# Forward and backward of a memory-augmented recurrent transformer block on one core: memory rows in another buffer, the last rest rows summed earlier, pinned GpSimd copies, one store on another queue

## Chip, core and metric

The kernel runs on one core of a Trainium2 chip. The metric is the device time of one execution in microseconds (us). Three executions of the kernel before took 2919.24, 2901.86 and 2914.58 us; their median is 2914.58 us. Three executions of one program thus lie up to 0.6% apart.

Engines are called as in the profile: PE is TensorE's matmul side, PEld its weight loads, DVE is VectorE, ACT is ScalarE, POOL is GpSimd, SP is SyncE. SP computes nothing here; it issues DMAs. POOL computes and also issues DMAs. Each engine takes its instructions strictly in the order in which they stand in its queue, so an instruction that waits holds up everything behind it.

## What is computed

One pre-LayerNorm block and the gradients of its inputs and weights, in bf16: 2048 tokens of width D = 448. The attention runs over 64 segments of 32 tokens, one after the other. Each segment sees its own tokens and 8 memory rows, and the first 8 output rows are the memory of the next segment. After that come a second LayerNorm and a SwiGLU feed-forward part (FFN) of width 1792.

```python
def _A_ref(x, mem0, Wq, Wk, Wv, Wo, seg_len):      # 16 heads of 256, M = 8, seg_len = 32
    mem = mem0
    for s in range(n_seg):                          # 64
        h = jnp.concatenate([mem, x[:, s*seg_len:(s+1)*seg_len, :]], axis=1)
        q, k, v = (jnp.einsum('btd,dhe->bhte', h, W) for W in (Wq, Wk, Wv))
        scores = jnp.where(mask, jnp.einsum('bhqe,bhke->bhqk', q, k) * scale, -1e9)
        o = jnp.einsum('bhqk,bhke->bhqe', _softmax(scores), v)
        o = jnp.einsum('bhte,hed->btd', o, Wo)
        mem = o[:, :M, :]
        outs.append(o[:, M:, :])
    return jnp.concatenate(outs, axis=1)
...
h  = x + _A_ref(_layernorm(x), mem0, Wq, Wk, Wv, Wo, 32)
h2 = h + (silu(_layernorm(h) @ w_gate) * (_layernorm(h) @ w_up)) @ w_down
# results: h2 and the gradients of x, mem0, Wq, Wk, Wv, Wo, w_gate, w_up, w_down for grad_out
```

## The kernel before

The program has four stages, which follow each other on PE. Their places in the profiled execution are: forward chain 0 to about 953 us, FFN forward and backward to about 1268, backward chain over the segments to about 2222, and the weight gradients (the tail) to the end.

A tile framework orders the instructions. It sorts by a priority, the chains stand in a high-priority block, and `tc.issue_after(ins)` puts an instruction no earlier than another one. The framework also adds the semaphore waits: for data, for a buffer that is still read or written, and for the semaphore of an earlier DMA, since each queue's DMAs take turns on eight semaphores.

**Forward chain** (lines 398 to 903). Each segment projects q, k and v, does the softmax and the output projection, and saves its tiles to DRAM. Some transposed weights are also made for later: `piece()` loads a block of a weight transposed into one of two staging buffers (`stg_b`), and `save()` notes a store of that buffer for later. `save_all(last)` issues the noted stores: on POOL's queue when `last` is None, else on SP's queue behind the segment's other stores. In the last segment (`end`) the two staging buffers are used once more, as `last_x`: `turned_by_pe` (line 618) turns the last token block on PE and copies four PSUM banks into them. The store that still reads one of them is that of a block of Wv turned (`Tv`, line 566). Also in the last segment, `_FFNLoads.at(0)`, `at(1)` and `at(2)` issue the loads of the FFN's weights on SP.

**FFN** (lines 906 to 1129). Eight iterations of two 128-token tiles. In each, PE does the gate, up and `dz` projections (`proj`, line 988), the down projection (1086), and the input gradient (1112). `sg` holds the sigmoids. POOL then makes `t1 = 1 - sg` over 3584 elements per partition (`k.pool_op`, line 1063), which DVE needs (1068, 1075) before its products (1093 to 1095), which in turn the matmuls of line 1112 read. `normed(n + 1)` (line 1011) prepares the next iteration: it normalises the rows (1018) and pads the loaded `grad_out` rows from 448 to 512 columns by a small copy on POOL (1020). `load_in` (299) fetches those rows on SP.

**Backward chain** (lines 1132 to 1600). 64 segments in reverse order, about 14 us each, in tiles t of four segments (r = s mod 4 runs 3, 2, 1, 0). What bears on the change:

- SP issues, in this order for each segment: the loads of the next one (`load_rest` 1201, `load_p` 1209, `load_v` 1213, `load_qk` 1221), then `own_saved` (1372), and once a tile, at r = 3, `prep_tile(t - 1)` (1170). `prep_tile` loads the output gradients of the next tile, turned, into the buffer `dhx`.
- The same buffer `dhx` also holds `rO`, and, once every 16 segments (jm == 0, that is s = 48, 32, 16 and 0), the rows of the memories' gradients, `rows` (line 1556). `memory_rows` (376) stores them by four DMAs on POOL's queue (381).
- A tile's rest rows (the first 8 of every segment) are projected as a list of small matmuls, `parts`, into the bank `pX`, copied to `om2`, summed over four groups of columns (`summed`, 1339; `rest_out`, 1356), copied to `pxs` and stored to `DXN` by four DMAs (`rest_sums_saved`, 1374).
- With all rows of `DXN` there, `norm_load` (1362), `norm_first` (1379) and `norm_second` (1392) do the LayerNorm's backward for the tile: loads of `DXN` into `om2`, of `XN` into `xn_t` and of `DH` into `dh_h`, then ACT and DVE work, and a store of `xn_t` to the result. `om2`, `xn_t` and `dh_h` are single buffers. `norm_first` writes a product it doesn't need into `prod_t`.
- After the loop, tile 1 and tile 0 are left (lines 1585 to 1595). Tile 1 goes through its LayerNorm part first; then tile 0's rest rows are summed and it goes through its own.

**Tail** (lines 1603 to 1810). Sums of outer products over all rows. The first group (`rows_by_d`, 1722) fills five `psf` banks and one `fx` bank with 20 matmuls each; ACT and DVE copy the banks out (lines 75 and 76), and the next group uses them again.

Of the kernel before, what the change touches and what calls it, by code (L numbers as in the profile page):

```python
# [10 lines left out]
BF16 = mybir.dt.bfloat16  # L11
# [379 lines left out]
def forward_chain(k: _K):  # L391
    nc, tc = k.nc, k.tc
    S, D, M, H, Dh, HD = k.S, k.D, k.M, k.H, k.Dh, k.HD
    SEG, L, NSEG, NT, KC, DP, MC, DC = k.SEG, k.L, k.NSEG, k.NT, k.KC, k.DP, k.MC, k.DC
# [39 lines left out]
    om = k.f32("f3", 256, "om")  # L434
# [134 lines left out]
    def save_all(last=None):  # L569
        for i in (1, 2):  # L570
            for fn in unsaved.pop((rot[0] + i) % 2, ()):
                if last is None:
                    fn()
                else:
                    with tc.issue_after(last.ins):
                        fn(nc.sync)
# [80 lines left out]
    def residual(t, h_t, x_t, last_v):  # L657
        with tc.issue_after(last_v.ins):
            nc.vector.tensor_tensor(out=h_t, in0=h_t, in1=x_t, op=ALU.add)
        nc.gpsimd.dma_start(out=dr["Hh"][t * P:(t + 1) * P, :], in_=h_t)  # L660
        st = smal.tile([P, nc.vector.BN_STATS_DIM], FP32, name="stats")
        with tc.issue_after(last_v.ins):
            nc.vector.bn_stats(out=st[:], in_=h_t)
        nc.vector.bn_aggr(out=k.mv2[:, t, :], in_=st[:])
# [7 lines left out]
    for s in range(NSEG):  # L672
        t, r = divmod(s, 4)
# [4 lines left out]
        xblk, om2 = xblk_b[t % 2], om_b[s % 2]  # L678
        end = s == NSEG - 1
        if due and jm % 3 == 1 and jm > 3:  # L680
            fetch(due[0], h_t, x2_t)
        with k.prio.crit():
# [146 lines left out]
            else:  # L829
                pm = k.ps1()  # L830
                for c in range(2):
# [3 lines left out]
                    out=hT_roll[:, :, (s + 1) % NWIN, SEG:L].rearrange("p (d c) m -> p d c m", d=2),  # L835
                    in_=pm[:, 0:32].rearrange("p (c d m) -> p d c m", c=2, d=2))
# [9 lines left out]
        for g in range(2):  # L846
            v_out = nc.sync.dma_start(out=dr["VG"][s, L * g:L * g + L], in_=Vs[64 * g:64 * g + L, :])
# [8 lines left out]
        if due and jm % 3 == 0 and jm > 5:  # L856
            n = due.pop(0)
            residual(n, h_t, x2_t, to_v)
        save_all(v_out)
        if (r == 0 and t > 0) or s == 2:  # L860
            prep_tile(t + 2)
        if s >= 4 and ((r > 0 and jm < 15) or (jm == 0)):
# [32 lines left out]
        elif jm == 15:  # L895
            for hf in range(2):
# [3 lines left out]
                                        in_=mh.rearrange("p c n -> p (c n)"))  # L900
# [10 lines left out]
def ffn_phase(k: _K, back):  # L911
    nc, tc = k.nc, k.tc
    S, D, F = k.S, k.D, k.F
    SEG, NT, KC, DP, FC = k.SEG, k.NT, k.KC, k.DP, k.FC
# [11 lines left out]
    h_b, dout_b, load_in = fl.h_b, fl.dout_b, fl.load_in  # L926
# [74 lines left out]
    last = NT // G - 1  # L1001
# [9 lines left out]
    def normed(n, after):  # L1011
        for tt in range(G):
            t = G * turns[n] + tt
            i = 2 * (n % 2) + tt
            for o, c0 in ((0, 0), (D, D - 64)):
                w = D if o == 0 else 64
                with tc.issue_after(after.ins):
                    nc.vector.tensor_scalar(out=hn_b[i][:, o:o + w], in0=h_b[i][:, c0:c0 + w], scalar1=mv2[:, t, 0:1],
                                            scalar2=rstd2[:, t:t + 1], op0=ALU.subtract, op1=ALU.mult)
            nc.gpsimd.tensor_copy(out=dout_b[i][:, D:DP], in_=dout_b[i][:, D - 64:D])  # L1020
            nc.gpsimd.dma_start(out=dr["HN"][t * P:(t + 1) * P, :], in_=hn_b[i][:, 0:D])

    def turned(n):
# [10 lines left out]
    for n, gi in enumerate(turns):  # L1034
# [44 lines left out]
        for tt in range(G):  # L1079
            t = G * gi + tt  # L1080
            rows = slice(t * P, (t + 1) * P)
# [20 lines left out]
        for tt in range(G):  # L1102
            t = G * gi + tt
            rows = slice(t * P, (t + 1) * P)
# [4 lines left out]
            i = 0  # L1109
# [16 lines left out]
        if n == last:  # L1126
            for tt in range(G):
                t = G * gi + tt
# [4 lines left out]
def backward_chain(k: _K):  # L1133
    nc, tc = k.nc, k.tc
    S, D, M, H, Dh, HD = k.S, k.D, k.M, k.H, k.Dh, k.HD
    SEG, L, NSEG, NT, KC, DP, MC, DC = k.SEG, k.L, k.NSEG, k.NT, k.KC, k.DP, k.MC, k.DC
# [5 lines left out]
    DQ = D // 4  # L1142
# [14 lines left out]
    dhx = A(59.8125, 4, P)  # L1157
    dOr = A(62.0625, 5, P)
    dxs, pxs = [x.bitcast(FP32) for x in (B(10.125, 2 * DQ), A(63.3125, 2 * DQ))]
# [92 lines left out]
    for c in range(4):  # L1252
        d0 = DQ * c
        while d0 < DQ * (c + 1):
            n = min(DQ * (c + 1), (d0 // P + 1) * P) - d0
# [11 lines left out]
    prod_t = k.f32("f2", D, "prod")  # L1267
    prod = prod_t[:, 0:8 * L].rearrange("p (h n) -> p h n", n=L)
    rO = dhx.rearrange("p c n -> p (c n)")
    om, om2 = k.f32("f1", 512, "om"), k.f32("f3", D, "om2")  # L1270
    dO_own = om[:].bitcast(BF16)
    pX, pD, pH = k.bank(6), k.bank(5), k.bank(7)
    with k.prio.crit():
        for b in range(2):
            pr, src = k.bank(b), (rO, A(46, 512))[b]
# [61 lines left out]
    def summed(ps, part):  # L1337
        for q in range(4):
            last = nc.tensor.matmul(ps[32 * q:32 * q + 32, 0:DQ], lhsT=sel[:], rhs=part[:, DQ * q:DQ * q + DQ],
                                    start=True, stop=True, skip_group_check=True)  # L1340
        return last

    parts = []

    def rest_parts(n):
        last = None
        for _ in range(min(n, len(parts))):
            last = parts.pop(0)()
        return last
# [6 lines left out]
    def rest_out():  # L1356
        summed(pX, om2)
        nc.scalar.copy(out=pxs, in_=pX[:, 0:DQ])
# [3 lines left out]
    def norm_load(t):  # L1362
        x = norm[t] = [om2, None]
        rows = slice(t * P, (t + 1) * P)
        nc.gpsimd.dma_start(out=x[0][:], in_=dr["DXN"][rows])
        nc.gpsimd.dma_start(out=xn_t, in_=dr["XN"][rows, 0:D])
        for c0 in (0, 224):
            nc.gpsimd.dma_start(out=dh_h[c0 // 224], in_=dr["DH"][rows, c0:c0 + 224])

    def own_saved(s):  # L1370
        r0 = 32 * s + M
        nc.sync.dma_start(out=dr["DXN"][r0:r0 + 32].rearrange("n (q d) -> q n d", q=4), in_=dxs)

    def rest_sums_saved(t):
        dst = dr["DXN"][t * P:(t + 1) * P].rearrange("(r n) (q d) -> q r n d", r=4, q=4)
        for q in range(4):
            nc.gpsimd.dma_start(out=dst[q][:, 0:M], in_=pxs[32 * q:32 * q + 32])

    def norm_first(t, after):
        x, rstd, junk = norm[t][0], k.rstd1[:, t:t + 1], prod_t  # L1380
        m1, m2 = [smal.tile([P, 1], FP32, name=f"lnb_m{i}") for i in (1, 2)]
        with tc.issue_after(after["s"].ins):
            nc.scalar.activation(out=x[:], in_=x[:], func=ACT.Copy, accum_out=m1[:])
        nc.vector.tensor_tensor_reduce(out=junk[:, 0:D], in0=x[:], in1=xn_t, scale=1.0, scalar=0.0,
                                       op0=ALU.mult, op1=ALU.add, accum_out=m2[:])
        m1s, m2s = [smal.tile([P, 1], FP32, name=f"lnb_m{i}s") for i in (1, 2)]
        nc.vector.tensor_scalar(out=m1s[:], in0=m1[:], scalar1=-1.0 / D, scalar2=rstd, op0=ALU.mult, op1=ALU.mult)
        nc.vector.tensor_scalar(out=m2s[:], in0=m2[:], scalar1=-1.0 / D, scalar2=None, op0=ALU.mult)
        nc.vector.scalar_tensor_tensor(out=x[:], in0=xn_t, scalar=m2s[:], in1=x[:], op0=ALU.mult, op1=ALU.add)
        norm[t][1] = m1s  # L1390

    def norm_second(t, after):
        x, m1s = norm.pop(t)
        with tc.issue_after(after["s"].ins):
            nc.scalar.activation(out=x[:], in_=x[:], func=ACT.Identity, scale=k.rstd1[:, t:t + 1], bias=m1s[:])
        for c0 in (0, 224):
            nc.vector.tensor_tensor(out=xn_t[:, c0:c0 + 224], in0=x[:, c0:c0 + 224], in1=dh_h[c0 // 224], op=ALU.add)
        nc.gpsimd.dma_start(out=OUT1[t * P:(t + 1) * P, :], in_=xn_t)

    V_FILL = {3: 16, 2: 16, 1: 16, 0: 3 * MC}  # L1400
    for s in range(NSEG - 1, -1, -1):
        t, r = divmod(s, 4)
# [14 lines left out]
        with k.prio.crit():  # L1417
# [6 lines left out]
            pool_op = nc.gpsimd.tensor_copy(out=doT[:, :, 0:M], in_=R4_b[t % 2][:, :, r * M:(r + 1) * M])  # L1424
# [78 lines left out]
            def first_rows(nm):  # L1503
                last = {}
                for b in range(3):
                    c0, n, v = c12(pps[nm][b], b)
                    with tc.issue_after(turned["vsv"[b]].ins):
                        last["vsv"[b]] = k.evac(lo[nm][:, c0:c0 + n, r * M:(r + 1) * M], v[:, :, 0:M], "vsv"[b])
                return last
# [8 lines left out]
            cast = first_rows("q")  # L1518
# [20 lines left out]
            pool_op = nc.gpsimd.tensor_copy(out=dmr[0:DQ, :, jm, :], in_=do_roll[0:DQ, :, sl, SEG:L])  # L1539
# [6 lines left out]
            if s > 0:  # L1546
# [3 lines left out]
                                      in_=pm[0:DQ, 0:P].rearrange("p (c n) -> p c n", n=32)[:, :, 24:32])  # L1550
# [2 lines left out]
                    nc.sync.dma_start(out=OUT2[:, DQ * q:DQ * q + DQ], in_=ot[32 * q + 24:32 * q + 32, :])  # L1553
            nc.scalar.copy(out=dxs, in_=pq[:, 0:DQ])
            if jm == 0:
                rows = dhx.rearrange("p c n -> p (c n)")
                k.evac(rows[:, 0:D], pr[:, 0:D], "s")
            if rest:
                k.evac(rO, pR[:], "s")
# [8 lines left out]
        if r == 0:  # L1568
# [10 lines left out]
            for fn, at in due:  # L1579
                if s == 0:  # L1580
                    k.last_stores.append(fn)
                else:
                    later(s - at[0], at[1], fn)
    own_saved(0)
    for t in (1, 0):
        if t == 0:
            rest_parts(len(parts))
            nc.scalar.copy(out=om2[:], in_=pX[:, 0:D])
            rest_out()
        with tc.issue_after(pool_op.ins):  # L1590
            rest_sums_saved(t)
            norm_load(t)
        norm_first(t, cast)
        norm_second(t, cast)
    assert not pending


# [243 lines left out]
```

## Time and profile before

| what | value |
|---|---|
| median of three executions | 2914.58 us |
| the profiled execution | 2902.99 us, of which the span in the trace is 2901.2 us |
| PE busy | 94% of the span, 41647 matmuls |
| DVE, ACT, POOL busy | 45%, 36%, 32% |
| DMA | 571.55 MB, 197 GB/s on average; the software queue (POOL's) 157.95 MB, the hardware queue (SP's) 407.32 MB |
| mean granted PE clock | 0.981 of full speed |

Times in the trace count from the start of the span. A line of a timeline gives the start, the time, the engine and source line, what it writes and reads, how many instructions were merged, and in brackets how long the engine had been idle and what ended that. A line of the list of waits gives who waited for whom, then the total in us, how often, and the longest wait. "SPq" is SP's DMA queue: the time there is how long SP took to issue.

### The profile page before, as it was taken

How to read it: one execution, taken by the hardware profiler on the slowest of the kernel's cores; microseconds unless marked ns; L12 is line 12 of the kernel's file. 1: busy time of each engine (PE TensorE's matmuls, PEld its weight loads, DVE VectorE, ACT ScalarE, POOL GpSimd, SP SyncE). 2: the span in 40 equal slices, each digit the busy share in tenths (PEclk: the TensorE clock that was granted, in tenths of full speed). 3: DMA queues.
4: the chain of work that ended last, by engine and by line, in shares of the span. 5: the costliest groups of instructions: out<-in, count | busy, mean ns of one | idle time of the engine just before them, and what ended most of it. 6: DMA issues, size and time to landing. Idle time of an engine off the chain costs nothing.

```text
span 2901.2 us, 98006 instructions
## 1 busy us (share of the span) xinstructions
PE 2737.4 (94%) x41647; PEld 1579.0 (54%) x41651; DVE 1306.1 (45%) x3352; ACT 1046.3 (36%) x2579; POOL 925.1 (32%) x2064
## 2 busy tenths in 40 slices
PE   5999999999999998989999999999998989999999
PEld 3565556565555555545565555555554444544444
DVE  4555565555555576645554554555553011111110
ACT  2555455455454444433333333333332011111110
POOL 1222232233222222423554544545543111111211
PEclk9999999999999999989999999999999999999999
DMA  7677778777777989995776777776778997969951
GB/s 259 149 190 196 193 189 200 192 191 198 202 184 213 290 202 225 213 301 142 172 186 173 177 175 179 179 180 166 179 171 264 322 248 159 215 175 229 184 165 52
DMA packets 781870, 571.55 MB, mean 197 GB/s; under 512 B 632432, under 2 KB 673688, under 8 KB 778872
## 3 DMA queue, kind: packets, MB, share of 16 engines
q1 hardware_dynamic: 717224, 407.32, 59.6%
q0 software_dynamic: 64208, 157.95, 17.3%
q8 instruction: 328, 5.37, 0.8%
q14 instruction: 110, 0.90, 0.1%
HBM read 181.58 MB, written 244.92 MB: 147 GB/s over the span
## 4 chain that ended last, share of the span: by engine, by line
PE 72%; DMA 10%; issue 7%; ACT 3%; DVE 3%; SPq 2%; POOL 2%; POOLq 0%; ACTq 0%; DVEq 0%
PE bank L1333 9%; PE psf L1682 8%; PE psf L590 6%; PE psf L725 5%; PE bank L1180 4%; PE po L772 4%; PE psf L988 3%; PE fx L1682 3%; PE bank L1298 2%; PE psf L614 2%; PE fx L1112 2%; PE bank L1353 2%; DMA arA<-VG 2%; PE bank L1439 2%; PE psf L506 2%
## 5 line engine op out<-in xcount | busy, mean ns | idle before, releaser
L75 DVE CAST arA<-psf 128x512 bf16<-128x512 f32 (+2 forms) x285 | 159.8, 561 | 487.6 <-PE psf L1682 249.9
L76 ACT CAST arA<-psf 128x512 bf16<-128x512 f32 (+3 forms) x379 | 189.7, 509 | 524.1 <-PE psf L1682 215.2
L1333 PE MATMUL bank<-arW,arA 128*32 128x448 bf16 x6144 | 319.6, 356 | 7.0 <-DMA arW<-Tq 3.6
L76 ACT CAST arA<-bank 128x96 bf16<-128x96 f32 (+4 forms) x608 | 193.5, 376 | 108.3 <-PE bank L1321 90.5
L1682 PEld LDWEIGHTS <-arA 128*128 128x128 bf16 x1440 | 139.4, 99 | 162.4 <-issue 7.7
L1682 PE MATMUL psf<-arW,arA 128*128 128x512 bf16 x882 | 224.4, 383 | 0.0
L1333 PEld LDWEIGHTS <-arA 128*32 128x32 bf16 x6144 | 155.4, 97 | 125.8 <-ACT arA L76 12.2
L725 PE MATMUL psf<-arW,arA 128*64 128x512 bf16 x1536 | 212.2, 382 | 0.0
L590 PE MATMUL psf<-arW,arA 128*32 128x512 bf16 x3072 | 189.8, 381 | 7.8 <-DVE arA L75 0.9
L988 PE MATMUL psf<-arW 128*128 128x256 bf16 (+1 forms) x1288 | 149.0, 277 | 5.9 <-DVE arA L75 4.6
L1759 POOL DMA_DIRECT2D out_dram<-arA x96 | 52.0, 542 | 261.6 <-DVE arA L75 234.9
L1210 POOL DMA_DIRECT2D arA<-P_all x256 | 127.7, 505 | 22.3 <-issue 17.9
L988 PEld LDWEIGHTS <-arW 128*128 128x128 bf16 (+1 forms) x1344 | 103.3, 97 | 57.8 <-issue 46.3
L75 DVE CAST arA<-bank 128x256 bf16<-128x256 f32 (+4 forms) x386 | 129.4, 389 | 9.1 <-PE bank L1180 4.2
L1180 PE MATMUL bank<-arW,arA 112*32 112x512 bf16 x2048 | 131.4, 400 | 1.6 <-DVE arA L1549 1.6
L772 PE MATMUL po<-arW,arA 128*32 128x256 bf16 (+1 forms) x4096 | 128.3, 263 | 1.2 <-DVE arA L75 1.2
L590 PEld LDWEIGHTS <-arA 128*32 128x32 bf16 x3072 | 70.3, 96 | 105.2 <-issue 28.5
L1722 PE MATMUL psf<-arW 128*128 128x448 bf16 x525 | 112.9, 357 | 5.1 <-DVE arA L75 5.1
L772 PEld LDWEIGHTS <-arA 128*32 128x32 bf16 x4096 | 104.7, 96 | 9.0 <-DVE arA L75 1.5
L1226 POOL COPY arB<-arB 40x320 bf16<-40x320 bf16 x128 | 64.4, 503 | 117.3 <-DMA arB<-P_all 81.8
L76 ACT CAST arB<-psf 128x64 bf16<-128x64 f32 (+1 forms) x192 | 65.1, 341 | 98.1 <-PE psf L597 75.7
L1112 PE MATMUL fx<-arW,arA 128*128 128x448 bf16 x448 | 89.2, 358 | 10.2 <-DVE arW L1088 10.2
(316 smaller groups left out, 5079.7 us busy)
## 6 DMA issues: line engine op xcount, KB each, us to landing
arW<-T SPq DMA_DIRECT2D x256, 128.0 KB
X_o<-arA SPq DMA_DIRECT2D x37, 512.0 KB
T<-arA SPq DMA_DIRECT2D x64, 256.0 KB
X_v<-arA POOLq DMA_DIRECT2D x30, 512.0 KB
X_k<-arA POOLq DMA_DIRECT2D x30, 512.0 KB, 4.5
X_q<-arA POOLq DMA_DIRECT2D x30, 512.0 KB, 3.2
out_dram<-arA POOLq DMA_DIRECT2D x84, 128.0 KB, 4.8
VG<-arA SPq DMA_DIRECT2D x64, 160.0 KB
```

The lines of the kernel that those rows point to most:

```text
L75: return nc.vector.tensor_copy(out=out, in_=in_)
L76: return nc.scalar.copy(out=out, in_=in_)
L590: nc.tensor.matmul(banks[b][w][32 * q:32 * q + 32, :], lhsT=hT_roll[:, kc, sl, M:L], rhs=(Wq_sb, Wk_sb)[w][:, kc, col(q, b)], start=(b == ...
L725: nc.tensor.matmul(pV[b][64 * g:64 * g + 64, 0:512], lhsT=hT_flat[:, kc, sl * L:sl * L + 64], rhs=Wv_sb[:, kc, n * 512:(n + 1) * 512], sta ...
L772: last = nc.tensor.matmul(pO[32 * q:32 * q + 32, 0:w], lhsT=xblk[:, j, r * SEG:(r + 1) * SEG], rhs=Wo_sb[:, cj(j), 256 * dh:256 * dh + w], ...
L988: nc.tensor.matmul(ps[fp][:, f2 * 256:(f2 + 1) * 256], lhsT=Wt[lo:hi, kc, c * P:(c + 1) * P], rhs=xT[lo:hi, kc, :], start=(kc == 0 and f2 ...
L1112: k.last_dh = nc.tensor.matmul(pdh[:, 0:D], lhsT=srcT[:, tt, c, :], rhs=WT[:, c, :], start=(i == 0), stop=(i == 2 * FC - 1))
L1180: last = nc.tensor.matmul(bank[32 * q:32 * q + 32, :], lhsT=lhs(c), rhs=WoT_sb[0:DQ, c, n0:n0 + 512], start=(c == 0), stop=(c == 3), skip_ ...
L1210: nc.gpsimd.dma_start(out=P4[32 * q:32 * q + 32, 2 * x + g], in_=pa[64 * g + M:64 * g + L, x])
L1333: last = nc.tensor.matmul(ps[32 * q:32 * q + 32, 0:D], lhsT=lhs(j), rhs=WT[:, cj(j), :], start=(start and i < 4), stop=(stop and i >= len( ...
L1682: k.last_mm = nc.tensor.matmul(pa[i][:, 0:w], lhsT=lhs_of(b)[:, i // 2 * P:(i // 2 + 1) * P], rhs=rhs_of(q, b, i % 2), start=(b == 0), sto ...
L1722: k.last_mm = nc.tensor.matmul(pa[i][:, 0:D], lhsT=lhs_of(b, i), rhs=rhs_of(b), start=(bi == 0), stop=(bi == m + 3))
```

## The change

Four edits in one diff:

1. The memory rows go into `om2` (seen as bf16) and no longer into `dhx`, except in segment 0. The four stores of `memory_rows` then read `om2`.
2. After the loop, the rest of `parts` is run first, `pX` is copied to `om` (no longer `om2`), summed, and copied to the first 112 columns of `prod_t`. Both tiles' rest sums are stored, tile 1's from `pxs` and tile 0's from `prod_t`. After that, both tiles go through their LayerNorm parts, pinned behind that last copy on ACT.
3. In the FFN, the padding copies of `normed(n)` for n > 0 are pinned behind POOL's `t1` operation of the iteration that calls them.
4. In the last forward segment `save_all` issues the noted store on POOL's queue and not behind the segment's stores on SP.

```diff
@@ forward_chain
-        save_all(v_out)
+        save_all(None if end else v_out)
@@ ffn_phase, normed(n, after)
-            nc.gpsimd.tensor_copy(out=dout_b[i][:, D:DP], in_=dout_b[i][:, D - 64:D])
+            with tc.issue_after(k.pool_op.ins) if n > 0 else nullcontext():
+                nc.gpsimd.tensor_copy(out=dout_b[i][:, D:DP], in_=dout_b[i][:, D - 64:D])
@@ backward_chain
-    def rest_sums_saved(t):
+    def rest_sums_saved(t, src=pxs):
         dst = dr["DXN"][t * P:(t + 1) * P].rearrange("(r n) (q d) -> q r n d", r=4, q=4)
         for q in range(4):
-            nc.gpsimd.dma_start(out=dst[q][:, 0:M], in_=pxs[32 * q:32 * q + 32])
+            nc.gpsimd.dma_start(out=dst[q][:, 0:M], in_=src[32 * q:32 * q + 32])
...
             if jm == 0:
-                rows = dhx.rearrange("p c n -> p (c n)")
+                rows = om2[:].bitcast(BF16) if s > 0 else dhx.rearrange("p c n -> p (c n)")
                 k.evac(rows[:, 0:D], pr[:, 0:D], "s")
...
     own_saved(0)
+    rest_parts(len(parts))
+    nc.scalar.copy(out=om[:, 0:D], in_=pX[:, 0:D])
+    summed(pX, om)
+    last = {"s": nc.scalar.copy(out=prod_t[:, 0:DQ], in_=pX[:, 0:DQ])}
+    for t, src in ((1, pxs), (0, prod_t[:, 0:DQ])):
+        with tc.issue_after(pool_op.ins):
+            rest_sums_saved(t, src)
     for t in (1, 0):
-        if t == 0:
-            rest_parts(len(parts))
-            nc.scalar.copy(out=om2[:], in_=pX[:, 0:D])
-            rest_out()
-        with tc.issue_after(pool_op.ins):
-            rest_sums_saved(t)
-            norm_load(t)
-        norm_first(t, cast)
-        norm_second(t, cast)
+        norm_load(t)
+        norm_first(t, last)
+        norm_second(t, last)
     assert not pending
```

## The prediction

> **What bounds the kernel now.** I read the page first, then PE's list of waits, then the timelines around each long wait.
>
> ```profile
> PE 2737.4 (94%) x41647; PEld 1579.0 (54%) x41651; DVE 1306.1 (45%) x3352; ACT 1046.3 (36%) x2579; POOL 925.1 (32%) x2064
> ...
> PE bank L1315 <- DMA arA<-P_all: 11.9, 6, 4.3
> PE fx L1112 <- DVE arW L1088: 10.2, 3, 7.3
> PE bank L1339 <- ACT om L1588: 7.9, 1, 7.9
> PE psf L1722 <- DVE arA L75: 5.1, 1, 5.1
> PE psf L988 <- DVE arA L75: 4.6, 1, 4.6
> ```
>
> PE bounds the kernel: it is idle for 2901.2 − 2737.4 = 164 us only. No edit removes matmuls, so all that can be won lies in these waits and in the slow clock behind them. The five are in the places that the change touches.
>
> **Memory rows.** This is the timeline of SP, POOL and PE around the end of segment 48.
>
> ```profile
> 1513.46 1.75 POOL L381 DMA_DIRECT2D DC<-arA  x3 [0.33 <-issue]
> ...
> 1516.42 0.58 SPq L1372 DMA_DIRECT2D DXN<-arB  x1
> 1520.43 1.22 SPq L1170 DMA_TRANSPOSE arA<-DHb  x1
> ...
> 1523.96 4.55 SPq L1209 DMA_DIRECT2D arA<-P_all  x8
> ...
> 1530.13 0.42 PE L1315 MATMUL bank<-arA 32*128 32x160 bf16 x2 [4.28 <-DMA arA<-P_all]
> ```
>
> SP is free at 1517.00, but `prep_tile` (1170) starts at 1520.43: it may not write `dhx` before the four stores of line 381 have read it. Behind it on SP stand the loads of the next segment, so PE waits 4.28 us for the P rows. The granted clock from 1531 to 1536 is then 0.50. By the starts of line 1545, segments 46, 30 and 14 take 20.63, 19.41 and 20.10 us, where an undisturbed one at r = 2 takes 13.74: 18.9 us lost in all. With the rows in `om2` SP's waits go (3.4, 2.5 and 3.4 us). The stores themselves stay, at the same place on POOL; `om2`'s next writer is the `DXN` load at 1523.74, after the stores have landed (5 to 6 us after issue), so nothing new waits there. PE's idle times of 4.28, 4.05 and 4.10 fall to about 0.9, 1.5 and 0.7, which is 3.1 us left. What is late next is the same load of P rows. Short gaps can cost clock too: after gaps of 0.91, 1.96 and 1.32 us (segments 24, 18, 7) the clock was 0.62, 0.71 and 0.64, and about 2.2 us more were lost; after 0.87 (segment 42) it stayed at 1.00. Of the three gaps left I count one as followed by such a loss, 2 us. **Gain 18.9 − 3.1 − 2 = 14 us**; ends 18.9 (no gap left) and 18.9 − 3.1 − 6.6 = 9.
>
> [...]
>
> **Pinned pool copies.** Timelines of POOL, DVE and PE in the FFN's fourth iteration:
>
> ```profile
> 1094.14 0.24 POOL L1020 COPY arW<-arW 128x64 bf16<-128x64 bf16 x1 [3.13 <-DMA arW<-in_grad_out_dram]
> 1094.34 3.17 POOL L1063 TENSOR_SCALAR arW<-arA 128x3584 bf16<-128x3584 bf16 x1
> ...
> 1097.55 2.03 DVE L1068 TENSOR_TENSOR arW<-arA,arW 128x3584 bf16<-128x3584 bf16 x1 [9.88 <-POOL arW L1063]
> ...
> 1105.23 7.50 PE L1112 MATMUL fx<-arW,arA 128*128 128x448 bf16 x28 [7.31 <-DVE arW L1088]
> ```
>
> The copies for the next iteration stand ahead of `t1` on POOL and wait for their load; `t1` was ready at about 1080.6, when ACT ended the sigmoids. Pinned behind it, `t1` ends near 1084, DVE's 1068 follows its own 1058 at 1087.7, the products start when ACT has the last `dz` (1093.1) and end before PE is through line 1086 (1097.9): no wait is left. That is 7.31 us, and 28 matmuls in 7.50 us instead of the 5.46 of other iterations, 2.04. Two more iterations have waits of 1.45 (at 1061.75 and 1180.27) with the same cause. Sum 12.2. The moved copies (0.24 us each, two per iteration) now hold up POOL's stores behind them; these wait for DVE until 8 to 11 us later anyway. PE turns the copied rows about 20 us after `t1`'s start. Against it: the FFN's DMA share is 0.9 to 1.1 in most stretches of 10 us, so a faster PE may meet later loads. I take off 3: **gain 9 us**, ends 4 and 12.
>
> **The store moved.** Timelines of SP, DVE and PE where the FFN begins:
>
> ```profile
> 947.56 11.71 SPq L845 DMA_DIRECT2D T<-q_st  x1
> ...
> 961.50 0.35 SPq L566 DMA_DIRECT2D Tv<-arA  x1
> ...
> 969.99 0.69 DVE L75 COPY arA<-psf 128x1024 bf16<-128x1024 bf16 x1 [5.23 <-DMA Tv<-arA]
> ...
> 970.73 12.77 PE L988 MATMUL psf<-arW 128*128 128x256 bf16 x90 [4.56 <-DVE arA L75]
> ```
>
> SP's queue is full of weight loads, so the store of 448 KB goes out at 961.50 and lands by 969.99; until then two PSUM banks can't be emptied and PE waits. As built, the store now stands on POOL ahead of the first padding copies, which waited until 939.01. It waits there for its transposed load (issued 932.79), so it is issued by 939.0. Stores of X_k (512 KB) land in 4.5 us, the HN stores of this window in 6.7: 943.5 to 945.7. The two copies out of PSUM move forward too, on DVE ahead of lines 664, 1007 and 1018, on ACT ahead of the square root; DVE gets there at 945.6. PE asks for 1018's rows at 953.3, and 1018 ends about 4.1 us after the landing (copy 1.01, table load 1.28, root 0.30, 1018's four 1.22), so a landing by 949.2 costs nothing. Won are 4.56 us and, at a clock of 0.50 from 971 to 976, 2.5: **gain 7 us**, ends 0 and 8. SP loses one issue of 0.35, and its T and VG stores are unmoved.
>
> **The end of the backward chain.** Timelines of PE, ACT and POOL:
>
> ```profile
> 2236.33 0.58 ACT L1383 ACTIVATE om<-om 128x448 f32<-128x448 f32 x1 [13.11 <-DMA om<-DXN]
> ...
> 2240.79 0.60 PE L1339 MATMUL bank<-om,sel 128*32 128x112 f32 x8 [7.93 <-ACT om L1588]
> ...
> 2248.51 0.59 POOL L1366 DMA_DIRECT2D arB<-XN  x1 [4.12 <-DMA out_dram<-arB]
> ...
> 2261.73 1.28 PE L1722 MATMUL psf<-arW 128*128 128x448 bf16 x3 [5.05 <-DVE arA L75]
> ```
>
> Now PE waits twice: 7.93 us for tile 0's `pX` copy, behind tile 1's LayerNorm part on ACT, and 5.05 for the first copies of the tail, behind tile 0's on both engines. The first wait goes. The tail's first 120 matmuls (0.19 each) then end near 2222.85 + 22.8 + 0.6 = 2246.3. But the copies out of their banks still stand behind tile 0's part, so the question is when that ends. Tile 1's `DXN` load is issued at 2230.96 as before. Behind it come four more stores, 0.6 each; the last, at 2233.3, lands 6.1 later (2243.8 to 2249.9 before), at 2239.4. They read `prod_t`, which tile 1's `norm_first` overwrites, so DVE waits until then rather than 2237.03: a new wait of 2.4 us, and the tail's copies queue behind it. Tile 1's result store moves from 2240.65 to 2243.05, lands 7.8 later (as before: 2248.5), and only then `XN` may be loaded into the same buffer, 5.1 us: 2256. From DVE's start (2258.00) to PE's resumption (2261.73) were 3.7: PE goes on at 2259.9 instead of 2261.73. One long wait replaces two. `XN` and `DH` of tile 1 load earlier, while POOL is idle. **Gain 2 us**; ends 5 (the store lands in 4.5, the median of its kind) and −1 (with the longest landings, 7.3 and 9).
>
> **Sum.** 14 + 9 + 7 + 2 = 32 us, 2903 − 32 = 2871 for an execution like the profiled one. That one (2902.99, 1.8 us more than its span) stands 11.6 below the median of 2914.58, so the forecast for the median is 2883.
>
> **Rivals.**
> *DMA holds the FFN* (chance 0.20). The share of 0.9 to 1.1 speaks for it; the stretches at 0.21 (1050 to 1060) and 0.51 (1200 to 1210), where SP had waited for gradient stores that POOL held back, against. If half of what the FFN parts win (16) is given back at the weight loads that open the backward chain (PE waited there 2.3 to 3.3 us at a time), the gain is 24: 2891.
> *The store lands no earlier* (0.08). The 16 DMA engines are busy at 1.03 to 1.08 from 940 to 970. If it still landed at 970, DVE would hold 1018 until about 974, and PE its first FFN transposes, 21 us later than 953.3; less 7 already lost there, the part costs 14 and the whole gains 11: 2904. The HN rows' 6.7 us speak against it. [...]
> *POOL is stuck behind the moved store* (0.03), the case that ends slower. The store waits at the head of POOL for its transposed load; line 855's copy (941.82), which PE's 876 needs at 944.8, stands behind it. From 944.8 on each us costs one, and beyond 944.8 + 32 = 977 the kernel is slower; at 990 it would take 2928. The longest such wait on SP was 4.2 us.
> *The forecast*: 0.65. The rest, 0.04, is noise on either side.
>
> **Numbers.** Low: all upper ends, 18.9 + 12 + 8 + 5 = 44, gives 2871; with the runs' scatter of about 8 below, 2860. High: the lower ends, 9 + 4 + 0 − 1 = 12, gives 2903, which also takes in the first two rivals; with some scatter 2907. About 1% (29 us, 2885.4) is what can be told from no change. The forecast lies just beyond it: of its 0.65 about 0.39 is faster by over 1%, of the first rival 0.06, of the rest 0.03. Faster 0.48, within 1% 0.48, slower 0.04.
>
> **What would show it.** Right: line 1170 right behind 1372 in segments 47, 31 and 15, and segments 46, 30 and 14 at 14 to 17 us; `t1` ahead of the copies and no wait over 1 us at 1112; line 566 on POOL near 939 and no wait of 4.56; in the tail no wait for the `pX` copy but one of over 10 us at 1722. Wrong: the weight loads at 1272 to 1297 waiting longer than before; PE's transposes of line 1029 later than 954; segments 46, 30 and 14 still near 20.

## The result and the profile after

| | before | changed |
|---|---|---|
| median, first comparison | 2911.97 us (4 runs) | 2870.27 us (4 runs) |
| ratio, 95% interval | | 0.9855 [0.9818, 0.9891] |
| median, second comparison | 2904.19 us (11 runs) | 2872.87 us (6 runs) |
| ratio, 95% interval | | 0.9891 [0.9854, 0.9929] |
| profiled execution | 2902.99 us | 2871.71 us, span 2869.9 us |
| granted PE clock | 0.981 | 0.988 |

The change makes the kernel faster by 1.1% to 1.5%. Between the two profiled executions lie 31.3 us, where the prediction had 32 for an execution like the profiled one. That they agree so closely is in part luck, as the part on the prediction shows.

The page of the changed kernel, and its list of what PE waited for:

```profile
PE 2727.5 (95%) x41651; PEld 1575.5 (55%) x41651; DVE 1308.1 (46%) x3352; ACT 1046.2 (36%) x2579; POOL 929.0 (32%) x2065
```

```profile
PE bank L1440 <- DMA arA<-VG: 8.9, 7, 2.5
PE bank L1316 <- DMA arA<-P_all: 8.9, 6, 2.5
PE psf L1724 <- DVE arA L75: 7.1, 1, 7.1
```

The lines of the changed program are 1 higher than before from line 1021 on, and 2 higher in the tail. Of the five waits shown before, those at 1112 (10.2 us), 1339 (7.9) and 988 behind DVE's copy (4.6) are gone. For the P rows (now 1316) the longest fell from 4.3 to 2.5, and the one at the tail's products (now 1724) grew from 5.1 to 7.1. The waits for the `VG` rows (now 1440) grew from 4.4 to 8.9 us in all. PE's idle time fell from 163.8 to 142.4 us (span less busy time). The other 10 of the 31 us are busy time: the same matmuls ran less often at half clock. PE was busy at a granted clock of 0.50 for 76.7 us before and for 53.7 after; half of the difference is 11.5 us.

**Memory rows.** SP, POOL and PE at the end of segment 48, in the timeline of the changed kernel:

```profile
1497.15 0.58 SPq L1373 DMA_DIRECT2D DXN<-arB  x1
1497.15 0.59 POOL L381 DMA_DIRECT2D DC<-om  x1 [0.21 <-issue]
...
1497.83 1.21 SPq L1171 DMA_TRANSPOSE arA<-DHb  x1
...
1508.44 0.29 PE L1316 MATMUL bank<-arA 32*128 32x160 bf16 x2 [0.57 <-DMA arA<-P_all]
```

The stores now read `om`. The transposed load (1171) starts 0.10 us after `own_saved` (1373) has been issued, although POOL issues its last store of memory rows (381) at that very time; before, 3.4 us lay between. PE waits 0.57 us rather than 4.28. A few us later it waits 1.90 for the `VG` rows, the next load on SP: that is what comes late next.

**Pinned copies.** POOL and PE in the FFN's fourth iteration:

```profile
1070.04 3.17 POOL L1064 TENSOR_SCALAR arW<-arA 128x3584 bf16<-128x3584 bf16 x1 [1.69 <-ACT arA L1054]
...
1087.17 3.00 PE L1113 MATMUL fx<-arW,arA 128*128 128x448 bf16 x15
1087.83 0.47 POOL L1021 COPY arW<-arW 128x64 bf16<-128x64 bf16 x1 [14.10 <-DMA arW<-in_grad_out_dram]
```

`t1` waits only for ACT: it starts 0.09 us after ACT has ended the sigmoids (1069.95); before, behind the copy that waited, 13.8 us lay between. The copy for the next iteration still waits 14.10 us for its load, but behind `t1`, and no bracket stands on PE's line.

**The store.** Its issue on POOL, a copy out of PSUM that needs it to have landed, the store on SP that had held it, and PE's products:

```profile
938.02 0.55 POOL L566 DMA_DIRECT2D Tv<-arA  x1 [6.29 <-issue]
...
945.31 0.69 DVE L75 COPY arA<-psf 128x1024 bf16<-128x1024 bf16 x1 [0.44 <-issue]
...
946.49 11.40 SPq L845 DMA_DIRECT2D T<-q_st  x1
...
955.25 19.28 PE L988 MATMUL psf<-arW 128*128 128x256 bf16 x168 [1.58 <-ACT arW L76]
```

The store was in DRAM by 945.31 at the latest, where it was issued at 961.50 before. All 168 products run without a break, behind a wait of 1.58 us for ACT; before, three shorter waits in these products took 1.3 us beside the 4.56.

**The end of the backward chain.** DVE, POOL and PE:

```profile
2212.61 0.62 DVE L1385 CUSTOM_DVE_ANT_0 prod<-om,arB 128x448 f32<-128x448 f32 x1 [3.51 <-DMA DXN<-prod]
...
2216.25 0.57 POOL L1399 DMA_DIRECT2D out_dram<-arB  x1
...
2221.39 0.54 POOL L1367 DMA_DIRECT2D arB<-XN  x1 [3.49 <-DMA out_dram<-arB]
...
2226.88 0.62 DVE L1385 CUSTOM_DVE_ANT_0 prod<-om,arB 128x448 f32<-128x448 f32 x1 [3.01 <-DMA arB<-XN]
...
2230.53 1.28 PE L1724 MATMUL psf<-arW 128*128 128x448 bf16 x3 [7.12 <-DVE arA L75]
```

This is the foretold chain, link by link: DVE waits for the new stores out of `prod_t` (3.51 us), tile 1's result must land (2216.25 to 2221.39) before `XN` of tile 0 may be loaded, and the copies that PE needs stand behind tile 0's part; the first on DVE start at 2229.86.

### The profile page after: what moved, and what is told of

It reads as the page before. It is cut to its first block, busy times and chain, and to the rows that moved or that the text cites. A ratio compares the mean times of both kernels' runs of the same rounds, so it can differ in the third digit from the quotient of the medians.

```text
span 2869.9 us, 98023 instructions
## 1 busy us (share of the span) xinstructions
PE 2727.5 (95%) x41651; PEld 1575.5 (55%) x41651; DVE 1308.1 (46%) x3352; ACT 1046.2 (36%) x2579; POOL 929.0 (32%) x2065
## 4 chain that ended last, share of the span: by engine, by line
PE 73%; DMA 10%; issue 8%; ACT 3%; DVE 3%; POOL 2%; SPq 1%; POOLq 0%; ACTq 0%; DVEq 0%
PE bank L1334 9%; PE psf L1684 8%; PE psf L590 6%; PE psf L988 5%; PE psf L725 4%; PE bank L1181 4%; PE po L772 4%; PE fx L1684 3%; PE bank L1299 2%; PE fx L1113 2%; PE psf L614 2%; DMA arA<-VG 2%; PE bank L1354 2%; PE bank L1440 2%; PE psf L506 1%
## 5 line engine op out<-in xcount | busy, mean ns | idle before, releaser
L725 PEld LDWEIGHTS <-arA 128*64 128x64 bf16 x1536 | 68.4, 109 | 52.8 <-issue 26.3
```

The source lines that it names most:

```text
L725: nc.tensor.matmul(pV[b][64 * g:64 * g + 64, 0:512], lhsT=hT_flat[:, kc, sl * L:sl * L + 64], rhs=Wv_sb[:, kc, n * 512:(n + 1) * 512], sta ...
```

## The experiments

Each kernel ran beside the kernel before on one chip. Whole times tell parts of 3 to 12 us apart only roughly (an interval is 12 to 22 us wide), so each part is also measured in the traces, over its own stretch: the three memory segments; the block from PE's last wait of 0.61 us at line 757 to the first start of line 1546 (1545 in some); PE's waits around the end of the chain.

### One part undone

Memory rows back in `dhx`:

```diff
-                rows = om2[:].bitcast(BF16) if s > 0 else dhx.rearrange("p c n -> p (c n)")
+                rows = dhx.rearrange("p c n -> p (c n)")
```

> The changed kernel with one part undone: the memory rows go back into dhx. My theory: the transposed load of DHb (line 1171) waits again for the four stores of line 381, 2.5 to 3.4 us at segments 47, 31 and 15, PE waits about 4 us for the P rows (line 1316), and segments 46, 30 and 14 take 19 to 21 us by the starts of line 1546, where the changed kernel had 17.39, 15.77 and 14.17. That is 13 us more in all, about 2884. Rival: the backward chain's gain is scatter of its clock and its transfers from run to run; then the three segments stay at 14 to 18 and the time near 2871.

Ratio to the kernel before 0.9928 [0.9901, 0.9955], median 2884.87 us. Segments 46, 30 and 14 took 19.14, 20.75 and 18.46 us. The same place in its timeline:

```profile
1494.51 0.58 SPq L1373 DMA_DIRECT2D DXN<-arB  x1
...
1498.57 1.21 SPq L1171 DMA_TRANSPOSE arA<-DHb  x1
...
1508.01 0.29 PE L1316 MATMUL bank<-arA 32*128 32x160 bf16 x2 [3.80 <-DMA arA<-P_all]
```

SP stands still for 3.48 us again, and PE waits for the P rows. The theory holds, with the last of the three segments a little under the 19 us expected.

Copies no longer pinned:

```diff
-            with tc.issue_after(k.pool_op.ins) if n > 0 else nullcontext():
-                nc.gpsimd.tensor_copy(out=dout_b[i][:, D:DP], in_=dout_b[i][:, D - 64:D])
+            nc.gpsimd.tensor_copy(out=dout_b[i][:, D:DP], in_=dout_b[i][:, D - 64:D])
```

> The changed kernel with one part undone: the padding copies (line 1020 here) are no longer held behind POOL's last operation. My theory: they stand ahead of t1 again and wait for the gradient load, PE waits up to 7 us at the products of line 1112 in the iteration whose load is late and 1 to 2 us in two others, 10 to 12 us in all: about 2882. Rival: with the Tv store early, the iterations run earlier against their loads, and no load is late; then only 0 to 4 us are lost and the pins earn little beside the store: about 2873.

Ratio 0.9935 [0.9912, 0.9957], median 2888.74 us. The block took 349.7 us, 12.5 more than the mean of the nine executions with both edits (337.2). The waits fell on two iterations, not on one large and two small ones, and around each the granted clock was 0.50 for 6.83 us. They are 4.95 us at 1019.42, and this, in the fourth:

```profile
1086.09 0.24 POOL L1020 COPY arW<-arW 128x64 bf16<-128x64 bf16 x1 [3.08 <-DMA arW<-in_grad_out_dram]
1086.29 3.17 POOL L1063 TENSOR_SCALAR arW<-arA 128x3584 bf16<-128x3584 bf16 x1
...
1097.17 4.26 PE L1112 MATMUL fx<-arW,arA 128*128 128x448 bf16 x11 [3.56 <-DVE arW L1088]
```

The store stays early here and PE waits all the same, so the rival falls: early or not, some load comes later than `t1` could start.

The `Tv` store back on SP (`save_all(v_out)`):

> The changed kernel with one part undone: the last segment's Tv store goes back to SP, where it stands behind a store that is held in the full queue. My theory: it is issued at about 961 and lands near 970, DVE's copy out of PSUM waits for that, PE waits about 4.6 us in the first products of the weight gradients (line 987 here) and then runs some us at half its clock: 7 us more, about 2878. Rival (the 16 DMA engines were the limit, not SP): landing and wait are as in the changed kernel, and the time stays near 2871.

Ratio 0.9893 [0.9861, 0.9924], median 2875.60 us.

```profile
944.07 12.11 SPq L845 DMA_DIRECT2D T<-q_st  x1
...
958.33 0.35 SPq L566 DMA_DIRECT2D Tv<-arA  x1
...
966.56 0.69 DVE L75 COPY arA<-psf 128x1024 bf16<-128x1024 bf16 x1 [4.74 <-DMA Tv<-arA]
...
967.31 12.36 PE L988 MATMUL psf<-arW 128*128 128x256 bf16 x90 [4.07 <-DVE arA L75]
```

Issue, landing and wait are back, each where expected within 4 us; the block took 342.7, 5.5 us more. The whole time alone (2.7 us over the changed kernel's second median) would not have shown it.

The tail's order as before:

> The changed kernel with one part undone: tile 0's rest rows are summed behind tile 1's LayerNorm part again. My theory: PE waits twice in the tail, 7 to 8 us for tile 0's sums and 4 to 6 us for the first copies, instead of once for 7.1 us: 4 us more, about 2875. Rival: the two orders cost the same, and the 4 us were the landing of one result store (5.1 us where 7.8 were expected); then one wait takes the place of two at no gain, and the time stays near 2871.

Ratio 0.9902 [0.987, 0.9935], median 2877.85 us. PE waited 7.44 us for tile 0's sums and 5.08 for the first copies, 12.5 in all. The new order has one wait, and it varies: 7.1, 9.3, 10.5, 9.9, 10.6 and 11.8 us in the six executions that have the part, 9.8 on average; four with the old order give 12.6. So the part wins 2.8 us in these waits. From the chain's last line 1546 to the end, the four executions with the old order take 685.5 us on average, five with the new one and nothing else changed in the tail 681.0. The 7.1 of the first profile was a lucky landing, as the rival had it in part.

### The changed kernel again, and the last LayerNorm part later

> The changed kernel once more, beside the next three on the same chip. By the parts measured in the traces (memory segments 11 to 13 us, the weight-gradient block 17 to 21, the tail's one wait for two 3 to 4) it should stand 31 to 38 us below the kernel before, a ratio of 0.987 to 0.989; if the first comparison's 0.9855 (42 us) is right, some 5 to 10 us come from a part that I haven't found.

Ratio 0.9891, 31.3 us: the low end of the gain that was expected. The 42 us of the first comparison need no hidden part; its four runs of the kernel before had a median 7 us above the 2905 that 21 later ones have. In this execution PE waits 1.88 us at the products (line 1113, at 1195.74), because DVE's line 1094 had waited 4.10 us for one of the FFN's own transposing DMAs. None of the eight other executions with both FFN edits has a wait over 0.6 us there.

Now tile 0's LayerNorm part behind the tail's first copies:

```diff
...
+    norm_load(0)
+    k.norm0 = lambda after: (norm_first(0, after), norm_second(0, after))
...
             j0 += n
+            if hf == 0 and j0 == 11:
+                k.norm0(k.last_ev)
```

> The changed kernel with the last LayerNorm part (tile 0's) put behind the copies of the tail's first eleven accumulators, on DVE and ACT. My theory: those copies stood behind the part, and it behind the load of XN, which waited for tile 1's result store; now PE's wait of 7 to 10 us at the tail's products (line 1724, here 1725) is gone, and the 2 us at half clock behind it: 9 us less than the changed kernel. Rival: the transfers pace the tail (the DMA share there is 1.03), so PE meets its next loads earlier, the waits at the transposes of the M rows (line 1665) grow by what was won, and the gain is 0 to 3.

Ratio 0.9869 [0.9835, 0.9903], median 2865.86 us. From the chain's last line 1546 to the end it took 670.3 us, where the five executions with the changed kernel's tail have 676.2 to 685.9 (mean 681.0). But PE still waits 5.19 us, for another reason:

```profile
2208.25 1.03 SPq L1575 DMA_DIRECT2D M_k<-arA  x1
...
2215.17 0.53 ACT L76 CAST arA<-psf 128x448 bf16<-128x448 f32 x1 [5.32 <-DMA M_k<-arA]
...
2215.76 2.40 PE L1725 MATMUL psf<-arW 128*128 128x448 bf16 x6 [5.19 <-ACT arA L76]
```

The tail's first results go into buffers from which segment 0's M rows are still being stored. Tile 0's LayerNorm part was the longer of two holds that overlap. The rival (later waits grow) fell: those at the M rows' transposes were 10.6 us, against 15.4 in the changed kernel beside it.

### Two waits that the change does not touch

The packing copies of the tail, held behind the copies out of PSUM (`evac` notes its instruction, behind which `pack` is pinned):

```diff
-                    k.evac(x_t[:, q * 1024:(q + 1) * 1024], pt[:, 0:1024])
+                    evac(x_t[:, q * 1024:(q + 1) * 1024], pt[:, 0:1024])
```

> The changed kernel with one thing changed that the change does not touch: in the tail, the copies that pack the M rows (lines 1656 and 1658) are held behind the copies out of PSUM of the transposes ahead of them. My theory: PE's waits at line 1665 (7.9 and 2.7 us, in three of the six profiled executions also 7 in the middle) come from DVE's copy out of PSUM standing behind a pack copy that waits for its M load; PE then has until the next transposes, some 6 us, and 5 to 10 us are won. Rival: PE waits for the same M load a little later, at the next transposes, and wins under 3.

Ratio 0.9831 [0.9799, 0.9863], median 2855.92 us. The tail took 666.4 us, 14.6 less than the mean of 681.0 and more than the 5 to 10 expected. Three waits at line 1665, 11.8 us in the first profile and 15.4 in the second, became one, so the rival falls:

```profile
2352.15 0.62 PE L1665 MATMUL ph<-ident,arA 128*128 128x128 bf16 x8 [2.56 <-DVE arA L1656]
```

> The edits of the two kernels before this one together. If the two waits are independent, 14 to 19 us less than the changed kernel; if the transfers pace the tail, PE arrives at the M loads 9 us earlier and waits for them longer, and the gain is 5 to 8.

Ratio 0.9813 [0.9778, 0.9848], median 2850.45 us. The tail took 658.9 us: 22.1 less than the changed kernel's mean, where the two alone took 10.7 and 14.6 off. They add up nearly in full. Each figure is of one execution, and the five without these edits spread over 9.7 us.

> The kernel with both edits of the tail (the last LayerNorm part late, the pack copies behind), and with the stores of the M rows of segment 0 ahead of those of its X rows on SP. My theory: the 5.2 us that PE still waits at line 1725 is for copies out of PSUM into buffers from which the M rows are being stored (DVE and ACT waited 7.6 and 5.3 us for the k rows, 4.2 and 4.4 for the v rows); stored first, they have landed by then, and 4 to 7 us are won over that kernel. Rival: the X rows' buffers are loaded over next, so the loads of the attention outputs come later by as much, PE waits for them, and nothing is won.

Ratio 0.9813 [0.9774, 0.9851], median 2849.17 us: no gain that the times can tell. The copies wait for the M rows still: DVE and ACT stand still for 8.14 and 8.85 us until the store of the v rows has landed. SP issues it at 2209.05 and it has landed by 2215.63, where in the kernel with the late LayerNorm part alone it was issued at 2212.83 and landed by 2220.11. Against the kernel with both edits, PE's wait fell from 5.15 to 2.96 us only, and the tail from 658.9 to 655.4. The theory names the right buffers, but it was wrong that the stores would have landed in time: SP issues the three of them from 2208.10 on, and the last needs 6.6 us. The rival's new waits for the attention outputs are 1.8 us in all. This kernel and the one with both edits have the lowest times of all.

### One group of parts alone

The FFN's two parts alone, on the kernel before:

> The kernel before with the pinned copies and the moved store only (memory rows in dhx, tail as before). From PE's last wait of 0.61 us at line 757 to the first start of line 1546 (here) the kernel before took 358.9 us, the changed one 337 to 338, without the pins 349.7, without the moved store 342.7. My theory: the two parts together win 21 us, of which 2 to 4 only together, as without both the waits fall on more iterations and the weight loads that open the backward chain come later: 337 to 339 here, 17 to 21 less than before in the whole, about 2885. Rival: the 358.9 was a bad execution, the parts win 12 and 5, and the whole stands 12 to 17 below before.

Ratio 0.9927 [0.9899, 0.9955], 19 us between the medians and 21 by the ratio. The block took 336.1 us; a second execution with neither part, that of the next kernel, took 355.8. So the two win 20 us together (nine executions with both have 336.1 to 339.0; those with neither 355.8 and 358.9) and 18 as the sum of each undone. The 2 us more together are within the scatter of the block. The rival (358.9 was a bad execution) fell.

The memory rows alone, on the kernel before:

> The kernel before with the memory rows in om2 only. My theory: segments 46, 30 and 14 take 45 to 50 us together, where they took 60.1, and the whole is 11 to 13 us shorter, a ratio of 0.9955 to 0.9965. Rival: what is won there is lost again at later loads in the chain, and the ratio is above 0.998.

Ratio 0.9959 [0.9938, 0.9981], 12 us. The three segments took 13.89, 17.33 and 14.07 us, 45.3 together. Over all executions they take 46.3 on average with `om2` (ten, 43.7 to 50.0) and 58.5 with `dhx` (three, 57.1 to 60.1): 12.2 us. The rival, that later loads take the gain back, is not wholly settled. From the first start of line 1546 (1545 in some) to the last, the chain takes 911.0 us on average with `om2` (903.3 to 915.7) and 920.3 with `dhx` (913.4 to 928.8), 9.3 us less. Whether the missing 3 us are given back or are scatter, these runs can't tell; the whole time's interval ends at 0.9981, where the rival had over 0.998.

## Why the prediction held, step by step

| part | forecast, us | measured, us |
|---|---|---|
| memory rows | 14 (9 to 18.9) | 12.2 (9.3 over the whole chain) |
| pinned copies | 9 (4 to 12); 12.2 before the deduction | 12.5 undone |
| store moved | 7 (0 to 8) | 5.5 undone |
| the last two together | 16 | 20 |
| end of the backward chain | 2 (-1 to 5) | 2.8 |
| sum | 32 | 35 (32 with 9.3) |

- **Memory rows.** The cause is shown: undone it comes back, alone it wins the same. The size is within 2 us in the three segments (within 5 over the whole chain). In the first profile 0.57 and 1.90 us of waits were left after segment 47, 1.87 (an issue, no load) after 31 and none over 0.5 after 15, where 0.9, 1.5 and 0.7 had been put. What stayed late there was the `VG` rows more than the P rows. In the second execution of the changed kernel the P rows were late as foretold, by 1.81 us after segment 47 and 2.45 after 31. The loss behind a slowed stretch, put at 2.2, is 1.7 in most cases (last section). The stores of line 381, put at 5 to 6 us, landed in 4.2 to 6.0, which changes nothing.
- **Pinned copies.** The working before the deduction, 12.2 us, was right in its mechanism. That undoing the part cost 12.5 is in part luck: the waits came back on two iterations with 8.5 us, not on three with 10.2. The step that failed is the 3 us taken off for DMA. In these two windows of the changed kernel's FFN (PE's busy time after the length, then the other engines; at the end of a line PE's clock, the DMA share and GB/s) the transfers run at 0.92 to 1.11, and PE doesn't wait:

```profile
980.00:1020.00 40.00, 40.00 (x292) 24.02 (x291) 30.53 (x53) 16.89 (x33) 13.47 (x21) 1.00 1.11 232
1020.00:1060.00 40.00, 40.00 (x304) 24.48 (x303) 28.55 (x53) 21.73 (x42) 10.70 (x15) 1.00 0.92 192
```

  A DMA share of about 1 did not mean here that PE's next load was late. The worry was not empty: the one wait of 1.88 us at line 1113 in nine executions was for a transfer. The weight loads that open the backward chain did not wait longer either (7.1 us at `To`, `Tv` and `Tq`; 9.3 before), so the first rival fell.
- **The store.** Its place, landing and wait are right: foretold to land between 943.5 and 945.7, there by 945.31. The rival with no earlier landing fell, and so did the one with POOL stuck: the store was issued at 938.02, foretold by 939.0. The HN rows, read as landing in 6.7 us there, take 7.7 in the trace, which moves the upper end to 946.7; the landing fits either. What was saved is the time that SP took to issue what stands ahead: counted from PE's last wait at line 757, the store went out 22.5 and 22.8 us earlier than in the two executions shown with it on SP, where SP spent some 18 us of that time issuing, 12.11 and 11.71 us of it on one store. From issue to landing it took at most 7.3 us on POOL, and at most 8.2 and 8.5 on SP. The size, 5.5 against 7, rests on one execution with this part undone.
- **End of the chain.** The mechanism is right in each link. The wait at 1722 (now 1724) was to be over 10 us, and is 9.8 on average. Not foreseen: the same copies also wait for segment 0's last stores, which is why removing the LayerNorm part from their path leaves 5.2.
- **The number.** 2883 against 2870.27 and 2872.87, within the range. The sum of the parts was good; the term that was off is the 11.6 us added for the median of three runs over the profiled execution. Later runs of the kernel before have a median of 2905, 2 above the profiled one. That median was scatter, not an offset. The 31.3 us between the two profiles is near 32 by luck: 21.0 of it lie in the FFN's block, 5.2 in the whole chain, 4.3 in the tail and 0.7 ahead of the block, where the forecast had 16, 14 and 2. The three segments won 12.8 there, but the rest of the chain took 7.6 more than in the profile before, which is within the scatter of that stretch (856 to 871 us over the thirteen profiles).

## What to carry to other kernels

Where a queue stands still, ask which buffer its head waits for and what stands behind it: three of the four parts moved one short operation, or its buffer, out of the way of work that didn't need it. An operation that waits for a load belongs behind the work that others wait for, in pinned order, as both the padding copies and the tail's packing copies show. To size parts of a few tenths of a per cent, compare the stretch of the trace that each touches over all the executions at hand, and take no offset from a median of three.

## What was not expected of the hardware

How a short gap on PE costs clock could be counted over the ten profiled executions before the last three kernels: all gaps of 0.5 us or more in the backward chain, from 1290 to 2190 us, with no other within 7 us. "Slowed" means a granted clock under 0.9 within 3 us after the gap.

| gap on PE, us | gaps | slowed |
|---|---|---|
| 0.5 to 0.9 | 65 | 0 |
| 0.9 to 1.4 | 27 | 5 |
| 1.4 to 2.0 | 22 | 11 |
| 2.0 to 2.6 | 8 | 6 |
| over 2.6 | 10 | 10 |

A slowed stretch runs at 0.50, and in 25 of the 32 cases it costs 1.64 to 1.71 us, which is 3.3 to 3.4 us at half speed; in the other seven, 2.6 to 3.4. The prediction had 2.2 from three cases. So in these executions a gap of 0.8 us costs itself, and one of 3 us nearly 5 or more. In the clock records of all thirteen traces, each of the 52 slowed stretches in the chain lasts 3.41 or 6.83 us: in the kernel before, from 1290 to 2190 us, four last 3.41 and three 6.83, and in the changed kernel five last 3.41. In the kernel before a gap of 0.91 us was enough once: PE went on at 1855.90, and the clock was 0.50 from 1856.93 to 1860.34.
